# Two groups of tiled matmuls given another place in the order of a recurrent-attention and SoLU kernel

## The chip, the cores and the metric

The kernel runs on one core of one Trainium2 chip. The metric is the device time of one launch in microseconds (us), the median of the runs shown. All arithmetic is in float32.

## What is computed

A gated linear recurrence over 768 tokens, for 4 batches of 8 heads of width 48, is followed by a feed-forward block on the 3072 resulting rows of width 384. The block projects to 1024 (`w_in`), weighs by a softmax, normalises, and projects back to 384 (`w_out`).

```python
for t in range(S):
    state = alpha[:, :, t, :, None] * state + np.einsum('bhd,bhe->bhde', k[:, :, t], v[:, :, t])
    y[:, :, t] = np.einsum('bhd,bhde->bhe', q[:, :, t], state)
...
h = x @ w_in
e = np.exp(h - h_max)
sm = e / (np.sum(e, axis=-1, keepdims=True) + 1e-09)
solu = h * sm
ln = (solu - mu) / np.sqrt(var + 1e-06) * g_ln
return ln @ w_out
```

## The kernel before

The 768 tokens are cut into G = 6 groups of 128. Within a group the recurrence is turned into matrix products: decayed queries times decayed keys give scores, the scores are masked, and the output y is the masked scores times the values plus a read of the state that the earlier groups left. A product of keys and values then brings the state forward to the next group.

The order of instructions is written out by hand, since the tile scheduler is set to manual. Each engine works off its own instructions in program order. From line 922 on, the kernel goes through periods g = 1 to 5, each of 8 steps s. In each step, the feed-forward block of group g is driven on by one eighth (`up(g, s)`: three matmuls from x through `w_in` into a bank `h`, line 394, then Exp on ScalarE at line 408, a product on VectorE at 409 and Square on ScalarE at 412), one half of a projection back of an earlier group is done (`down`, eight matmuls, line 507), and the parts of the attention of group a = g + 1 are put in between. Dictionaries say which part goes where: `first` for period 1 and `usual` for periods 2, 3 and 4 (period 5 has no attention left). The places in a step are, in order: head, then `up` and `finish` (the output of a projected block: small sums on VectorE, a power on GpSimd at line 546, the scaled copy on ScalarE at 548, the store on SP at 549), then `next_state` and `token_sums` where step 0 has them, then behind, `running` (sums kept by VectorE and GpSimd, line 427), middle, `down`, tail.

The parts that matter here:

- `read_state(half)`, called "read0" and "read1" in the plans: half of the read of the state, 32 matmuls of 64 rows by 32 columns of the array (line 333, from `state` and the queries `q64` in the tile `lot`) into four banks y of PSUM.
- `read_values(a)`, "values": 64 matmuls of 128 rows by 32 columns (line 333, from masked scores `sT` and values `vn`) into the same banks; after them four copies on ScalarE (line 363) bring y into `x`, which `up(a, 0)` reads.
- `next_state(a)`, "kv": 64 matmuls of 128 rows by 32 columns (line 371, keys `kg` and values `vn`) into two of the banks that y had; then two sums on VectorE (line 381) into `state`.
- `token_sums(g - 1)`: 16 matmuls of 128 rows by 32 columns (line 462), the row sums of the feed-forward block's running sums, then a transposition and small sums on VectorE (lines 467 to 473).
- `down` and `up` use the whole array, 128 rows by 128 columns.

An instruction in float32 shows as two matmul records in the trace, so `up` is 6 records, `down` 8 for a half (it issues four instructions of 128 by 385), a half read 64, values 128, kv 128, the row sums 32.

In the kernel before, for periods 2, 3 and 4, read0 is in the middle of step 6, read1 in the tail of step 6 (behind `down`), and values in the middle of step 7 (behind `up(g, 7)`). In period 1, read1 and values already stand together in the middle of step 7. `next_state(1)` and `next_state(2)` are called at step 0 of their own periods, behind `up(g, 0)`; `next_state(3)` and `next_state(4)` are called as "kv" in the tail of step 7 of periods 2 and 3, behind `down` and ahead of the next period's `up(g, 0)`. `load_v(a)`, four loads on SP into `vn` (line 176), stands behind step 0, so it comes after the product that reads the values of the group before.

Of the kernel before, what the change touches and what calls it, by code (L numbers as in the profile page):

```python
# [32 lines left out]
def fast_path(ctx, tc, q, k, v, alpha, moe_w_in, moe_w_out, moe_g_ln, out):  # L33
# [97 lines left out]
    def load(src, dst, g):  # L131
        t = slice(g * P, (g + 1) * P)
        for b in range(B):
            nc.sync.dma_start(
                out=dst[32 * b : 32 * b + 32].rearrange("t h u d -> t h (u d)"),
                in_=src[b, :, t, :].rearrange("h (t u) d -> t h (u d)", u=TQ),
            )
# [35 lines left out]
    def load_v(g):  # L173
        t = slice(g * P, (g + 1) * P)
        for b in range(B):
            nc.sync.dma_start(out=held(vn, b), in_=v[b, :, t, :].rearrange("h p d -> p h d"))

    def firsts(src, dst):
        nc.vector.transpose(out=dst.rearrange("p h (t u) -> p h u t", u=TQ), in_=src[:, :, :, 0:E0])  # L179

    def lasts(src, dst):
        nc.vector.transpose(
            out=dst.rearrange("p j (i t u) -> p u j i t", u=TQ, i=2),
            in_=src[:, :, :, E0:D].rearrange("p (j i) u d -> p u j i d", i=2),
        )

    def alpha_T(g):
        nc.gpsimd.memset(aT[:, :, 0:1], 0.0)
        firsts(an, aT[:, 0:H, 1:SW])
        lasts(an, aT[:, H:NB, 1:SW])  # L190
# [15 lines left out]
    def scan_back(g, i):  # L206

        part = slice(NP * i, NP * i + NP)
        scan(h4[:, part], aT[:, part], unit, True)

    def inverses(g):
        nc.gpsimd.tensor_copy(out=fend[:, g], in_=h4[:, :, 1])  # L212
        nc.vector.reciprocal(out=seed[:, :, 0:1], in_=h4[:, :, 1:2])

    def scan_on(g, i):
        part = slice(NP * i, NP * i + NP)
        scan(aT[:, part], aT[:, part], seed[:, part], False)

    def keys_T(g):
        firsts(kn, kT[:, 0:H])  # L220
        lasts(kn, kT[:, H:NB])

    def keys(g):
        for part in (slice(0, H), slice(H, NB)):
            nc.gpsimd.tensor_tensor(out=kT[:, part], in0=kT[:, part], in1=hk[:, part], op=ALU.mult)  # L225

    def move_lasts():

        for b in range(B):
            i, c = divmod(b, 2)  # L230
            for k in range(2):
                nc.sync.dma_start(out=q64[64 * i + E0 : 64 * i + 64, c, k::2], in_=qe[32 * b : 32 * b + 32])

    def move_firsts():
        for b in range(B):
            i, c = divmod(b, 2)
            nc.sync.dma_start(out=q64[64 * i : 64 * i + E0, c], in_=qv[32 * b : 32 * b + 32, 0:H])

    def ends_of_decay():
        nc.gpsimd.tensor_copy(out=qe[:, :, P:SW], in_=h4[:, H:NB, 1:2])  # L240
        nc.gpsimd.tensor_copy(out=qv[:, 0:H, P:SW], in_=h4[:, 0:H, 1:2])

    def apart():
        for i in range(2):
            nc.scalar.mul(
                out=qv[:, H : 2 * H, 0:P].rearrange("p (j i) t -> p j i t", i=2)[:, :, i], in_=qe[:, :, 0:P],
                mul=parity[:, i : i + 1],
            )

    def queries(i):  # L250
        part = slice(NP * i, NP * i + NP)
        q = qe[:, :, 0:P] if i == 2 else qv[:, part, 0:P]
        nc.gpsimd.tensor_tensor(out=q, in0=q, in1=aT[:, part, 1:SW], op=ALU.mult)

    def decay(g):

        if g == 0:
            return
        for c in range(2):
            x = held(state, c)  # L260
            nc.gpsimd.tensor_tensor(  # L261
                out=x, in0=x, in1=q64[:, c, :, P:SW].to_broadcast([P, H, D]), op=ALU.mult
            )
# [22 lines left out]
    def masked(half, batches=range(B)):  # L286
        a = masks[half]
        for b in batches:
            nc.vector.tensor_tensor(  # L289
                out=sT[:, b, half * NP : half * NP + NP], in0=a[b], in1=mask[:, None, :].to_broadcast([P, NP, P]),  # L290
                op=ALU.mult,
            )
# [7 lines left out]
    def keys_back(g, t=None):  # L300
        t = t or banks("tp", [NP, P], 3)
        for j in range(NB):
            nc.tensor.transpose(out=t[j // NP][:, j % NP], in_=kT[:, j], identity=ident)
        for i in range(2):
            nc.scalar.copy(
                out=kg[:, :, NP * i : NP * i + NP, 0:E0].rearrange("p b j d -> p j b d"),
                in_=t[i].rearrange("p j (b d) -> p j b d", b=B),
            )
        for m in range(2):
            nc.scalar.copy(  # L310
                out=kg[:, :, m::2, E0 + E1 * m : D + E1 * m].rearrange("p b j d -> p j b d"),
                in_=t[2].rearrange("p j (b k d) -> p j b k d", b=B, k=2)[:, :, :, m],
            )
# [521 lines left out]
    for i in range(3):  # L835
# [11 lines left out]
    usual = dict(  # L847
        head={4: "keys_back", 5: "masked0", 6: "masked1"},
        behind={0: "v keys", 1: "on2 on0 on1", 2: "lasts firsts", 3: "apart", 5: "decay", 6: "alpha", 7: "back"},
        middle={6: "begin read0", 7: "values"},  # L850
        tail={4: "scores0", 5: "scores1", 6: "read1", 7: "kv"},
    )
    first = dict(
        head={3: "keys_back"},
# [4 lines left out]
        tail={6: "begin read0"},  # L859
        middle={7: "read1 values over"},  # L860
    )

    def attend(a, what):

        more = a + 1 < G
        if what == "v":
            load_v(a)
        elif what == "keys":
            keys_T(a)
            keys(a)  # L870
            if more:
                load(k, kn, a + 1)
        elif what[:2] == "on":
            if what == "on2":
                inverses(a)
            scan_on(a, int(what[2]))
        elif what == "lasts":
            lasts(qn, qe[:, :, 0:P])
            ends_of_decay()
            queries(2)  # L880
            move_lasts()
        elif what == "firsts":
            firsts(qn, qv[:, 0:H, 0:P])
            queries(0)
            queries(1)
            move_firsts()
            if more:
                load(q, qn, a + 1)
        elif what == "apart":
            apart()  # L890
        elif what == "decay":
            decay(a)
        elif what == "keys_back":
            if more:
                keys_back(a)
        elif what[:6] == "scores":
            scores(a, int(what[6]))
        elif what[:6] == "masked":
            masked(int(what[6]))
        elif what == "alpha" and more:  # L900
            alpha_T(a + 1)
            if a > 2:
                attend(a, "over")
        elif what == "over" and more:
            alpha_over(a + 1)
            if a + 2 < G:
                load(alpha, an, a + 2)
        elif what == "back" and more:
            for i in range(3):
                scan_back(a + 1, i)  # L910
        elif what == "begin":
            read_begin()
        elif what[:4] == "read":
            read_state(int(what[4]))
        elif what == "values":
            read_values(a)
        elif what == "kv" and more:
            next_state(a)

    centres = {4: (0, 1), 6: (2, 3), 7: (4, 5, 6, 7)}  # L920
# [1 line left out]
    for g in range(1, G + 1):  # L922
        rise, att = g < G, g + 1 < G
        plan = first if g == 1 else usual

        def at(where, s):
            for what in plan[where].get(s, "").split() if att else ():
                attend(g + 1, what)

        after = 3 if g == 1 else None  # L930
        if not rise:
            break
        for s in range(FC):
            at("head", s)
            if rise:
                up(g, s)
            if after is not None:
                finish(after)
                after = None
            if s == 0 and g < 3:  # L940
                next_state(g)
            if s == 0 and g > 1:
                token_sums(g - 1)
            at("behind", s)
            for f in centres.get(s, ()) if g == 1 else ():
                centre(f)
            if rise and s:
                running(g, s)
            at("middle", s)
            if s == FC - 1 and g < G - 1:  # L950
                todo.append((g * B, 0))
            if todo:
                n, half = todo.pop(0)
                down(n, half)
                if half:
                    after = n
            at("tail", s)
        if after is not None:
            finish(after)
        todo = [(n, half) for n in range(g * B, g * B + B) for half in range(2)][g < G - 1 :]  # L960
# [493 lines left out]
```

## Time and profile before

| | |
|---|---|
| median of 3 runs | 368.86 us (368.79 to 369.36) |
| the profiled execution's own time | 369.21 us |
| its span, first to last instruction | 367.4 us |
| TensorE (PE) busy | 359.7 us, 98% |
| VectorE (DVE), ScalarE (ACT), GpSimd (POOL) busy | 245.4, 146.1, 131.1 us |
| `down`, line 507, all periods | 384 records, 134.0 us |
| `up`, line 394, all periods | 288 records, 132.1 us |
| values, line 333 | 768 records, 22.6 us |
| read of the state, line 333 | 640 records, 11.6 us |
| kv, line 371 | 640 records, 7.8 us |

How to read it: the profile is of one execution, and its span leaves out 1.8 us of that execution's own time, which lie around the first and the last instruction. A line of the list in order of time gives the start of a group in us from the span's start, its length, the engine, the source line, the tile written and those read, then for TensorE the rows and columns of the array that are used (128\*128 is the whole array), the shape of the moving operand, and the number of records. What stands in brackets at the end is the time that the engine sat idle before, and who ended it. PEld is TensorE's weight load, listed as an engine of its own. Matmuls are pipelined and their ends are modelled, so the starts are the firm numbers.

### The profile page before, as it was taken

The page shows a single profiled execution, that of the slowest core. Times are in us where ns is not written, and L with a number is a line of the kernel's source. Part 1 is how long each engine was busy: PE and PEld are TensorE (multiplying, and loading weights), DVE is VectorE, ACT ScalarE, POOL GpSimd, SP SyncE. Part 2 cuts the span into 40 slices and gives each one's busy share as a digit, 9 for nine tenths or more (in the row PEclk, how much of TensorE's full clock was granted, in tenths as well). Part 3 has the DMA queues.
Part 4 walks back from the last instruction along what each step waited for, and adds up shares of the span by engine and source line. Part 5 has one row for each costly group of instructions (what it writes and reads, how often), then busy time and mean ns, then how long its engine had stood idle before and what let it go on. Part 6 is the DMA issues. An engine that isn't in the chain of part 4 may idle for free. (4 is left out here: it accounts for less than half of the span.)

```text
span 367.4 us, 10036 instructions
## 1 busy us (share of the span) xinstructions
PE 359.7 (98%) x4341; PEld 215.9 (59%) x4341; DVE 245.4 (67%) x375; ACT 146.1 (40%) x260; POOL 131.1 (36%) x129
## 2 busy tenths in 40 slices
PE   8999999999999999999999999999999999999994
PEld 8885355676755566566575556574556565555552
DVE  0999999979998787936575935665956314345420
ACT  2647878282645262251432252431242132222110
POOL 7020000004449944763133764232774121233300
PEclk9999999999999999999999999999999999999999
DMA  9996986335196419363135354004042000000011
GB/s 181 186 317 181 220 269 130 87 82 144 53 229 146 105 29 184 77 154 86 33 80 118 75 129 118 4 23 87 21 101 60 2 23 0 24 21 22 23 46 51
DMA packets 72871, 36.06 MB, mean 98 GB/s; under 512 B 48232, under 2 KB 70000, under 8 KB 72816
## 3 DMA queue, kind: packets, MB, share of 16 engines
q1 hardware_dynamic: 71792, 34.39, 39.8%
q10 hardware_dynamic: 1024, 0.92, 0.8%
q8 instruction: 36, 0.59, 0.7%
q14 instruction: 19, 0.16, 0.1%
HBM read 25.30 MB, written 4.72 MB: 82 GB/s over the span
## 5 line engine op out<-in xcount | busy, mean ns | idle before, releaser
L507 PE MATMUL o<-w_out,room 128*128 128x385 f32 x384 | 134.0, 492 | 0.0
L394 PE MATMUL h<-x,w_in 128*128 128x512 f32 x288 | 132.1, 598 | 0.5 <-DVE g_col L642 0.5
L507 PEld LDWEIGHTS o<-w_out,room 128*128 128x128 f32 x384 | 71.0, 190 | 54.7 <-issue 13.1
L394 PEld LDWEIGHTS h<-x,w_in 128*128 128x128 f32 x288 | 52.9, 189 | 58.2 <-issue 49.1
L409 DVE TENSOR_TENSOR room<-h,e 128x512 f32<-128x512 f32 x40 | 27.5, 688 | 73.7 <-ACT e L408 73.7
L408 ACT ACTIVATE e<-h 128x512 f32<-128x512 f32 x40 | 24.0, 599 | 100.6 <-PE h L394 100.6
L427 POOL TENSOR_TENSOR p<-p,e 128x512 f32<-128x512 f32 x30 | 42.7, 1423 | 20.0 <-ACT e L408 19.9
L412 ACT ACTIVATE u<-room 128x512 f32<-128x512 f32 x40 | 25.2, 630 | 39.3 <-DVE room L409 39.3
L546 POOL TENSOR_TENSOR r<-sums,mhalf 128x1 f32<-128x1 f32 x20 | 14.8, 739 | 72.9 <-DVE sums L537 72.7
L289 DVE TENSOR_TENSOR sT<-a,mask 128x512 f32<-128x512 f32 x43 | 26.7, 683 | 7.7 <-PE a L278 7.6
L204 DVE TENSOR_TENSOR_SCAN hT<-aT,unit 128x516 f32<-128x516 f32 x18 | 24.0, 1376 | 8.1 <-ACT aT L703 8.1
L204 DVE TENSOR_TENSOR_SCAN aT<-aT,seed 128x516 f32<-128x516 f32 x18 | 27.4, 1551 | 0.2
L427 DVE TENSOR_TENSOR p<-p,u 128x512 f32<-128x512 f32 x30 | 23.1, 768 | 5.1 <-ACT u L412 5.1
L225 POOL TENSOR_TENSOR kT<-kT,hT 128x1024 f32<-128x1024 f32 (+1 forms) x8 | 14.2, 1796 | 32.6 <-DVE kT L179 32.6
L278 PEld LDWEIGHTS a<-qv,kT 32*128 32x128 f32 x704 | 21.4, 186 | 7.4 <-issue 2.4
L278 PE MATMUL a<-qv,kT 32*128 32x128 f32 x704 | 23.9, 278 | 0.9 <-DVE qv L721 0.4
L212 POOL COPY fend<-hT 128x12 f32<-128x12 f32 x6 | 3.0, 507 | 56.1 <-DVE hT L204 56.1
L333 PE MATMUL y<-sT,vn 128*32 128x128 f32 x768 | 22.6, 273 | 0.2 <-DVE sT L289 0.2
L333 PEld LDWEIGHTS y<-sT,vn 128*32 128x32 f32 x768 | 20.7, 110 | 3.3 <-issue 2.7
L196 ACT ACTIVATE sq<-an,mone 128x1536 uint8<-128x1536 f32 x12 | 18.9, 1573 | 0.2
L548 ACT ACTIVATE o_sb<-o,r 128x384 f32<-128x384 f32 x16 | 9.3, 581 | 18.7 <-POOL r L546 18.7
L261 POOL TENSOR_TENSOR state<-state,lot 128x384 f32<-128x384 f32 x10 | 8.8, 900 | 12.0 <-DMA lot<-qv 11.8
(148 smaller groups left out, 375.8 us busy)
## 6 DMA issues: line engine op xcount, KB each, us to landing
vn<-in_v_dram SPq DMA_DIRECT2D x24, 192.0 KB, 4.6
an<-in_alpha_dram SPq DMA_DIRECT2D x20, 192.0 KB, 3.8
out_dram<-o_sb SPq DMA_DIRECT2D x20, 192.0 KB, 1.9
room<-in_moe_w_out_dram SPq DMA_DIRECT2D x8, 384.0 KB, 5.0
kn<-in_k_dram SPq DMA_DIRECT2D x16, 192.0 KB, 4.8
qn<-in_q_dram SPq DMA_DIRECT2D x16, 192.0 KB, 3.8
lot<-qe SPq DMA_DIRECT2D x40, 64.5 KB, 2.1
lot<-qv SPq DMA_DIRECT2D x20, 129.0 KB, 2.4
```

What stands on the lines that cost most here:

```text
L196: nc.scalar.activation(out=sq, in_=x, func=AF.Relu, scale=sign, bias=mone, accum_out=over[:, g, i : i + 1])
L204: nc.vector.tensor_tensor_scan(out=o, data0=a, data1=s, initial=1.0, op0=ALU.mult, op1=ALU.add)
L278: nc.tensor.matmul(a[b][:, i], lhsT=kT[quarter(b), kb], rhs=qv[quarter(b), qb, 0:P], start=not last and not i, stop=bool(last), tile_posit ...
L289: nc.vector.tensor_tensor(out=sT[:, b, half * NP : half * NP + NP], in0=a[b], in1=mask[:, None, :].to_broadcast([P, NP, P]), op=ALU.mult,)
L333: nc.tensor.matmul(y_bank(b)[quarter(r), a], lhsT=lhsT, rhs=rhs, start=(b, r) not in begun, stop=stop, tile_position=(row, 32 * r), skip_g ...
L394: nc.tensor.matmul(h, lhsT=w_in[:, a, f * P : (f + 1) * P], rhs=d["x"][:, a].rearrange("p b t -> p (b t)"), start=(a == 0), stop=(a == KC ...
L408: nc.scalar.activation(out=e, in_=h, func=AF.Exp)
L409: nc.vector.tensor_tensor(out=u, in0=h, in1=e, op=ALU.mult)
L412: nc.scalar.activation(out=u2, in_=u, func=AF.Square)
L427: eng.tensor_tensor(out=p, in0=d[0][i] if f == 1 else p, in1=d[f][i], op=ALU.add)
L507: nc.tensor.matmul(d["o"][:, 0 : DM + 1], lhsT=u_of(g, f)[:, b * P : b * P + P], rhs=w_out[:, f], start=(f == 0), stop=(f == FC - 1), skip ...
L546: nc.gpsimd.tensor_tensor(out=r, in0=s[:, 3:4], in1=mhalf, op=ALU.pow)
```

## The change

In the plan `usual`, "read1" goes from the tail of step 6 to the middle of step 7, right ahead of "values". So in periods 2, 3 and 4 the second half of the read comes behind `down` of step 6 and `up(g, 7)`. For group 4 alone, `next_state` is no longer called in the tail of step 7 of period 3 but at step 0 of period 4, behind `up(4, 0)` and right ahead of `token_sums(3)`. No instruction is added, removed or changed in shape.

```diff
     usual = dict(
         head={4: "keys_back", 5: "masked0", 6: "masked1"},
         behind={0: "v keys", 1: "on2 on0 on1", 2: "lasts firsts", 3: "apart", 5: "decay", 6: "alpha", 7: "back"},
-        middle={6: "begin read0", 7: "values"},
-        tail={4: "scores0", 5: "scores1", 6: "read1", 7: "kv"},
+        middle={6: "begin read0", 7: "read1 values"},
+        tail={4: "scores0", 5: "scores1", 7: "kv"},
     )
...
-        elif what == "kv" and more:
+        elif what == "kv" and more and a != 4:
             next_state(a)
...
-            if s == 0 and g < 3:
+            if s == 0 and g in (1, 2, 4):
                 next_state(g)
             if s == 0 and g > 1:
                 token_sums(g - 1)
```

## Prediction

> **What bounds the kernel now.** I read first the page's share of each engine, then TensorE's list in order of time over the later periods, then the same list where period g=1 ends, then ScalarE's and GpSimd's lists around one seam.
>
> ```profile
> PE 359.7 (98%) x4341; PEld 215.9 (59%) x4341; DVE 245.4 (67%) x375; ACT 146.1 (40%) x260; POOL 131.1 (36%) x129
> ```
>
> TensorE is busy all the time and nothing else is near it; the wait table gives it 0.2 to 1.1 us at seven places, none of them after 114 us. So the end moves one for one with the time from one TensorE group's start to the next group's start. I use starts throughout, since the ends are modelled and overlap the next start by 0.07 to 0.17 us.
>
> The seam of g=3 into g=4, before the change:
>
> ```profile
> 231.99 1.16 PE L333 MATMUL y<-lot,state 64*32 64x128 f32 x64
> 233.08 2.86 PE L507 MATMUL o<-w_out,room 128*128 128x385 f32 x8
> 235.87 1.16 PE L333 MATMUL y<-lot,state 64*32 64x128 f32 x64
> 236.96 2.84 PE L394 MATMUL h<-x,w_in 128*128 128x512 f32 x6
> 239.73 3.70 PE L333 MATMUL y<-sT,vn 128*32 128x128 f32 x128
> 243.36 2.86 PE L507 MATMUL o<-w_out,room 128*128 128x385 f32 x8
> 246.15 1.57 PE L371 MATMUL kv<-vn,kg 128*32 128x48 f32 x128
> 247.65 2.84 PE L394 MATMUL h<-x,w_in 128*128 128x512 f32 x6
> 250.42 0.65 PE L462 MATMUL rows<-p,ones 128*32 128x64 f32 x32
> 251.00 2.86 PE L507 MATMUL o<-w_out,room 128*128 128x385 f32 x8
> 253.70 2.74 PE L394 MATMUL h<-x,w_in 128*128 128x512 f32 x6
> 256.28 2.76 PE L507 MATMUL o<-w_out,room 128*128 128x385 f32 x8
> ```
>
> The fifth column is the shape of the array: 128*128 is whole, 64*32 or 128*32 is tiled. Look at how a whole-array group's length depends on its neighbours. Up (L394) takes 256.28 - 253.70 = 2.58 between two whole groups, 2.77 between two tiled ones (236.96 to 239.73, 247.65 to 250.42). Down (L507) takes 2.79 between two tiled ones (233.08, 243.36), 2.70 with only the group ahead tiled (251.00), and 2.59 to 2.60 between whole ones (the same list at 256.28 and 261.44). Each border between shapes costs about 0.1 us at either side of a whole group.
>
> Where g=1 ends, the kernel of before already has both orders that the change makes:
>
> ```profile
> 127.12 1.16 PE L333 MATMUL y<-lot,state 64*32 64x128 f32 x64
> 128.21 3.70 PE L333 MATMUL y<-sT,vn 128*32 128x128 f32 x128
> 131.84 2.86 PE L507 MATMUL o<-w_out,room 128*128 128x385 f32 x8
> 134.54 2.74 PE L394 MATMUL h<-x,w_in 128*128 128x512 f32 x6
> 137.21 1.57 PE L371 MATMUL kv<-vn,kg 128*32 128x48 f32 x128
> 138.59 0.64 PE L462 MATMUL rows<-p,ones 128*32 128x64 f32 x32
> 139.16 2.86 PE L507 MATMUL o<-w_out,room 128*128 128x385 f32 x8
> ```
>
> The read takes 1.09 with values behind it, as against 1.09 with up behind it (235.87 to 236.96); values take 3.63 in both places. The product kv takes 1.38 ahead of the row sums and 1.50 ahead of up.
>
> **What the Trainium skill says.** TensorEngine Tiling (Array Packing), section Key Properties: "Mode switching requires drain", a change of the tiling mode and not of the tile. It gives no price; this trace agrees and gives about 0.1 us at each side of a whole group. TensorE: Matmul & The Clock Gate, section Step-by-step: what each phase is for, says that TensorE pulls a weight load ahead of matmuls in flight. The list of weight loads agrees: between whole groups the load of up starts at 253.38, 0.32 ahead of its matmul at 253.70; behind a tiled group it starts together with its matmul, at 236.96; so what a border costs may be this lead. Perfetto Trace Analysis, section Identifying the Most-Contended Engine, says that TensorE's busy share is a poor measure because matmuls are pipelined: the 98% does not say that nothing can be gained, and indeed the same six matmuls take 2.58 or 2.77.
>
> **Part 1: the read of the state moved behind up of step 7** (periods g=2, 3, 4). Nothing is added or removed: 64 matmul records (32 instructions) trade places with the 6 of up. Before, from the start of down at step 6 to the end of values: 2.79 + 1.09 + 2.77 + 3.63 = 10.28, and the window sums show 10.28 for 177.16:187.44, 233.08:243.36 and 287.69:297.97 alike. After: down with a tiled group ahead and a whole one behind, 2.70 (251.00 and 131.84); up with a whole one ahead and a tiled one behind, 2.67 (134.54); read ahead of values, 1.09; values 3.63. Sum 10.09. Gain 0.19 each, 0.57 for three. It is free of new waits if up can start 1.18 earlier (1.09 + 0.09): its bank h was given up by step 5, and its Exp sat idle 2.44 us waiting for it at 239.84. VectorE sat idle 3.52 before its product at 240.47. What read waits for (queries in q64, the state decayed by GpSimd) is older still than for the first read. Values come no earlier relative to the masks; DVE's masks precede the first read anyway, since both use the same banks.
>
> **Part 2: next_state(4) moved out of step 7 of g=3 to behind up of step 0 of g=4**, once. Before, from the start of down to the end of the row sums: 2.79 + 1.50 + 2.77 + 0.58 = 7.64 (243.36 to 251.00; also 7.64 at 187.44 to 195.08). After it is the order at g=2, step 0: 2.70 + 2.67 + 1.38 + 0.57 = 7.32 (131.84 to 139.16). Gain 0.32.
>
> What else moves with it: two VectorE sums L381 (0.55 each) now stand behind the product L409 of up and ahead of the transposition of the row sums, as at 138.00, 138.78 and 139.72, where TensorE lost nothing. The state is wanted next by decay at step 5. On SP the four loads of v for period 5 wait for kv to have read vn: their issue slips from 247.66 by about 2.5 us relative to the seam (kv ends 6.75 behind the end of values instead of 4.29). Behind them on SP is the output store issued at 259.78, 6 us past their new end, and values want vn only at 294. GpSimd's queue keeps its order.
>
> The cover that gets thinner is x. Up of step 0 needs the four ScalarE copies of y (L363), and kv no longer stands between:
>
> ```profile
> 243.13 0.58 ACT L548 ACTIVATE o_sb<-o,r 128x384 f32<-128x384 f32 x1 [1.31 <-POOL r L546]
> 243.61 1.61 ACT L363 COPY x<-y 128x384 f32<-128x384 f32 x4
> ```
>
> The copies end at 245.22, 1.86 behind the end of values, held up by an output step that waits for GpSimd's 1.40 us power. Up will now come 2.70 behind the end of values instead of 4.29. That still leaves 0.84; and since up of step 7 runs 1.18 earlier against values, its whole chain (Exp, product, finish, power, output) does too, so the copies should end some 0.6 behind values and the slack be near 2. At g=4 the kernel of before already starts up 2.70 behind values (297.97 to 300.67), copies ending 1.06 behind, without a wait. I take nothing; from below it cannot be a gain, and from above, if all ScalarE work slipped by 1.5 us, it would cost 0.7.
>
> **Sum.** 0.57 + 0.32 = 0.89. Starts are read to 0.01, four seams of two readings each: 0.85 to 0.93. Behind each seam every group goes on at its usual length up to the last store, with no wait that could swallow the gain. The profiled execution took 369.21 for a span of 367.4, so it would become 368.32 with a span of 366.5; the median before is 368.86, 0.35 under that execution, so the forecast median is 367.97. That is 0.24% off, and this kernel's times can tell about 0.2% (0.74 us) from no change, so the sign is surer than the class.
>
> **The rivals.**
> - The borders save less where they now stand (64*32 straight into 128*32 is read from one place only, g=1, with both groups there under other loads), or x costs some: half to two thirds of the sum, 368.3 to 368.4. For it: one sample per new order. Against: the old orders repeat to 0.01 in three periods, so lengths hardly depend on what other engines do.
> - Up of step 0 waits for x at the seam from g=3 to g=4, and the end is later. Place: L394 at step 0 of g=4. Price: one for one past 2.70 behind values, so the copies would have to end 2.70 + 0.89 + 0.74 = 4.33 behind values to make it slower by 0.2%; then 369.6 or more. For it: ScalarE's output step there waits on a GpSimd power of 1.40 us beside VectorE's scans (0.55 at g=4). Against: it takes 2.5 us more than now, and the chain starts 1.18 earlier.
> - The change does not do what it says: the program's order of instructions has the moves on TensorE and on VectorE (L381) and none on GpSimd or SP; the time would stay 368.86. Very unlikely.
>
> **How the numbers follow.** Forecast 0.80, part of the gain 0.15, waiting for x 0.03, no effect 0.02. The forecast falls on the near side of 0.74 in about one of eight medians (the three before spread over 0.57): 0.70 of faster, 0.10 of same. Same adds the partial case and no effect less a little for noise: 0.26. Slower 0.04. The range runs from 367.5 (0.89 and a low median) to 368.65, which takes in the partial case.
>
> **What would show it.** Right: in g=2, 3, 4 the order down, up, read, values with 2.70, 2.67, 1.09, 3.63; at g=4 step 0 up, kv, rows with 2.67, 1.38, 0.57; span near 366.5. Wrong: up of step 0 in g=4 starting more than 2.71 behind values; the read longer than 1.10 ahead of values; a new TensorE wait in the table; or a later group longer than before, so that the gain is given back.

## The result and the profile after

The changed kernel took 368.08 us (median of 12 runs, 367.89 to 369.74) against 368.90 for the kernel before (12 runs, 368.77 to 370.30). The ratio is 0.9978, with a 95% interval of 0.9969 to 0.9987: 0.22% faster, and by that interval between 0.13% and 0.31%. Timed once more in the last group of experiments (label e12_changed_again), the ratio was 0.9971 (0.9960 to 0.9982). So it is faster by both intervals; whether by more than the 0.2% at which the forecast drew its line they leave open.

The profiled execution took 367.97 with a span of 366.2. TensorE's list in order of time shows the seam of g=3 into g=4 as it now is; the columns are those shown before.

```profile
231.53 1.16 PE L333 MATMUL y<-lot,state 64*32 64x128 f32 x64
232.63 2.86 PE L507 MATMUL o<-w_out,room 128*128 128x385 f32 x8
235.32 2.74 PE L394 MATMUL h<-x,w_in 128*128 128x512 f32 x6
237.99 1.16 PE L333 MATMUL y<-lot,state 64*32 64x128 f32 x64
239.08 3.70 PE L333 MATMUL y<-sT,vn 128*32 128x128 f32 x128
242.71 2.86 PE L507 MATMUL o<-w_out,room 128*128 128x385 f32 x8
245.41 2.74 PE L394 MATMUL h<-x,w_in 128*128 128x512 f32 x6
248.07 1.57 PE L371 MATMUL kv<-vn,kg 128*32 128x48 f32 x128
249.47 0.65 PE L462 MATMUL rows<-p,ones 128*32 128x64 f32 x32
250.05 2.86 PE L507 MATMUL o<-w_out,room 128*128 128x385 f32 x8
```

From start to start (down is line 507, up 394, kv 371, the row sums 462): down 2.69, up 2.67, read 1.09, values 3.63, together 10.08 in place of 10.28; then down 2.70, up 2.66, kv 1.40, row sums 0.58, together 7.34 in place of 7.64. In period 2 the first sum is 10.09 (176.90 to 186.99), in period 4 it is 10.08 (286.74 to 296.82); both were 10.28 before.

ScalarE's list around the same seam, for the cover of x:

```profile
241.39 0.58 ACT L548 ACTIVATE o_sb<-o,r 128x384 f32<-128x384 f32 x1 [1.31 <-POOL r L546]
241.87 1.61 ACT L363 COPY x<-y 128x384 f32<-128x384 f32 x4
```

The copies end at 243.48, 0.77 behind the end of values, and up follows at 245.41, 2.70 behind: no wait.

To compare single executions I use one stretch in what follows: from the start of the row sums of period 2 to the start of the last matmul of down. All that the change moves lies inside it, and the loads at the start lie outside; in every trace kept here the granted clock is 1.00 all through it. It was 223.41 us before and is 222.52 now: 0.90 less by the unrounded figures. The two spans differ by 1.24. Of the rest, 0.25 came earlier than 127 us and 0.09 behind the last matmul of down; nothing is changed in either place, so I take it for a difference between two executions.

### The profile page after: what moved, and what is told of

Read it like the earlier page. It is cut to its first block, busy times and chain, and to the rows that moved or that the text cites. A ratio compares the mean times of both kernels' runs of the same rounds, so it can differ in the third digit from the quotient of the medians.

```text
span 366.2 us, 10036 instructions
## 1 busy us (share of the span) xinstructions
PE 357.8 (98%) x4341; PEld 215.0 (59%) x4341; DVE 245.0 (67%) x375; ACT 146.4 (40%) x260; POOL 132.2 (36%) x129
## 5 line engine op out<-in xcount | busy, mean ns | idle before, releaser
L427 POOL TENSOR_TENSOR p<-p,e 128x512 f32<-128x512 f32 x30 | 43.7, 1458 | 20.0 <-ACT e L408 19.9
```

The costliest lines, as they stand in the source:

```text
L427: eng.tensor_tensor(out=p, in0=d[0][i] if f == 1 else p, in1=d[f][i], op=ALU.add)
```

## Experiments

The theory under test is the border theory: what counts is how often TensorE passes between groups of different array shape. The first rival is that up's earlier start did it; the others are waits (for x, or at the row sums). All experiments were timed against the kernel before on the same chip; the table gives each one's stretch too, which is that of a single execution.

| run | median us | ratio to before, 95% interval | stretch us |
|---|---|---|---|
| changed kernel | 368.08 | 0.9978 (0.9969 to 0.9987) | 222.52 |
| e1_read_alone | 368.51 | 0.9984 (0.9976 to 0.9991) | 222.82 |
| e2_kv_alone | 368.74 | 0.9991 (0.9981 to 1.0001) | 223.10 |
| e3_values_split | 369.13 | 1.0001 (0.9993 to 1.0009) | 223.51 |
| e4_rows_first | 368.20 | 0.9968 (0.9956 to 0.9981) | 222.52 |
| e5_kv3 | 368.14 | 0.9969 (0.9955 to 0.9982) | 222.26 |
| e6_reads_joined | 368.38 | 0.9978 (0.9970 to 0.9986) | 222.59 |
| e7_x_uncovered | 369.14 | 1.0000 (0.9990 to 1.0010) | 223.35 |
| e8_all_joined | 368.26 | 0.9974 (0.9964 to 0.9983) | 222.93 |
| e9_joined_34 | 367.48 | 0.9951 (0.9936 to 0.9966) | 221.44 |
| e10_shifted | 368.95 | 0.9997 (0.9985 to 1.0009) | 223.07 |
| e11_alpha_later | 368.21 | 0.9977 (0.9966 to 0.9988) | 222.92 |
| e12_changed_again | 368.26 | 0.9971 (0.9960 to 0.9982) | 222.58 |

### Each part alone

Part 1 alone (to the kernel before):

```diff
-        middle={6: "begin read0", 7: "values"},
-        tail={4: "scores0", 5: "scores1", 6: "read1", 7: "kv"},
+        middle={6: "begin read0", 7: "read1 values"},
+        tail={4: "scores0", 5: "scores1", 7: "kv"},
```

> Part 1 alone: the second read moved ahead of values in periods 2, 3 and 4, the product kv for group 4 left where it was. Border theory (what counts is how often TensorE goes between whole-array and tiled groups, about 0.10 us at each side of a whole group and 0.11 at the end of a tiled one): 10.28 becomes 10.09 in each of the three periods, 0.57 us less than before, nothing at the seam from g=3 to g=4 (7.64 stays). Earlier-start theory (the gain comes from step 7's up starting 1.2 us earlier for ScalarE and VectorE, the order of shapes being idle): no number for TensorE's groups, which would keep 2.79, 2.77 and 1.09, and a gain only where a wait was, so 0.

Part 2 alone (to the kernel before):

```diff
-        elif what == "kv" and more:
+        elif what == "kv" and more and a != 4:
...
-            if s == 0 and g < 3:
+            if s == 0 and g in (1, 2, 4):
```

> Part 2 alone: kv for group 4 behind up of step 0 and ahead of the row sums, the read left in step 6. Border theory: 7.64 becomes 7.32 at the seam from g=3 to g=4, 0.32 us less than before, 10.28 stays in all three periods; and the four copies of x end about 1.86 us behind values, so up at 2.70 behind still does not wait. Waiting-for-x theory: without part 1 the cover of x is thinner, up starts later than 2.71 behind values, and the gain is below 0.32.

The stretch became 0.59 and 0.31 shorter, for 0.57 and 0.32 expected, and the two add up to the 0.90 of both. In e1, TensorE had no wait before or after the change in these periods and still gained, which the earlier-start theory can't give.

TensorE's list of e2, from the end of values:

```profile
243.83 2.86 PE L507 MATMUL o<-w_out,room 128*128 128x385 f32 x8
246.53 2.74 PE L394 MATMUL h<-x,w_in 128*128 128x512 f32 x6
249.19 1.57 PE L371 MATMUL kv<-vn,kg 128*32 128x48 f32 x128
250.58 0.64 PE L462 MATMUL rows<-p,ones 128*32 128x64 f32 x32
251.15 2.86 PE L507 MATMUL o<-w_out,room 128*128 128x385 f32 x8
```

Up of step 0 came 2.70 behind values (243.83 to 246.53), so the smaller cover of x was enough even without part 1. By the times alone, part 2 would not be told from no change (the interval reaches 1.0001); the trace shows it (7.32 from 243.83 to 251.15, where it was 7.64).

### A border put back

```diff
-        middle={6: "begin read0", 7: "read1 values"},
+        middle={6: "begin read0", 7: "read1 values01"},
...
+        elif what == "values01":
+            read_values(a, (0, 1))
...
-                down(n, half)
+                if s == FC - 1 and att and g > 1:
+                    down(n, half, (0, 1))
+                    read_values(g + 1, (2, 3))
+                    down(n, half, (2, 3))
+                else:
+                    down(n, half)
```

> The changed kernel with a border put back: in step 7 of periods 2, 3 and 4, values of batches 0 and 1, half of down, values of batches 2 and 3, the other half of down. Same instructions, one more trip from tiled to whole and back in each period. Border theory: 0.10 + 0.10 at the whole group and 0.11 at the end of the tiled one, 0.31 us each, 0.94 in all above the changed kernel, so about 369.0, level with before. Earlier-start theory: no instruction of up moves, so nothing, 368.1.

TensorE's list of that kernel, from values to up of step 0:

```profile
239.16 1.96 PE L333 MATMUL y<-sT,vn 128*32 128x128 f32 x64
241.04 1.56 PE L507 MATMUL o<-w_out,room 128*128 128x385 f32 x4
242.53 1.95 PE L333 MATMUL y<-sT,vn 128*32 128x128 f32 x64
244.42 1.56 PE L507 MATMUL o<-w_out,room 128*128 128x385 f32 x4
245.82 2.74 PE L394 MATMUL h<-x,w_in 128*128 128x512 f32 x6
```

The same matmuls took 6.66 (239.16 to 245.82) where the changed kernel needs 6.33 (239.08 to 245.41). The two halves of values take 1.88 and 1.89, 0.14 more than the whole; the two halves of down 1.49 and 1.40, 0.19 more. Three times 0.33 is 0.99, and the stretch is 0.99 longer; the time is back level with before. No instruction of up was moved, so the earlier-start theory can't explain the loss; with e1 it has fallen.

### The same borders in another order

```diff
-            if s == 0 and g in (1, 2, 4):
+            if s == 0 and g in (1, 2):
                 next_state(g)
             if s == 0 and g > 1:
                 token_sums(g - 1)
+            if s == 0 and g == 4:
+                next_state(g)
```

> The changed kernel with the row sums ahead of kv at step 0 of period 4 in place of behind it. The same borders in another order. Border theory: the same time as the changed kernel, up 2.67, row sums about 0.46 (no border behind them), kv 1.50 (a border behind it), their sum 1.95 as before. A theory by which kv has to stand ahead of the row sums (its banks, or the sums' wait for the running sums of step 7): a wait of TensorE there, and longer.

TensorE's list of that kernel:

```profile
248.13 0.65 PE L462 MATMUL rows<-p,ones 128*32 128x64 f32 x32
248.60 1.54 PE L371 MATMUL kv<-vn,kg 128*32 128x48 f32 x128
250.07 2.86 PE L507 MATMUL o<-w_out,room 128*128 128x385 f32 x8
```

The stretch is the same to 0.01. The row sums take 0.47 with kv behind them (248.13 to 248.60) in place of 0.58, and kv 1.47 with down behind it in place of 1.40: the end of a tiled group costs about 0.1 when the next group has another array shape, and whichever of the two is last pays it. It is the adjacency that counts and not the place of kv.

### The cover of x

In period 3 down of step 7 is left out of its place and called in period 4 behind up of step 0:

```diff
             if rise:
                 up(g, s)
+            if g == 4 and s == 0:
+                down(3 * B, 0)
...
-                down(n, half)
+                if not (g == 3 and s == FC - 1):
+                    down(n, half)
```

> The changed kernel with the cover of x taken away at the seam from g=3 to g=4: down goes behind up of step 0, so that values are followed at once by up. The shapes and their borders are as many as before. Wait-for-x theory: up starts when the fourth copy of x is done, about 0.77 us behind values plus up to 0.1, so some 0.8 to 0.9 us longer than the changed kernel. No-wait theory: the same time.

TensorE's list of that kernel:

```profile
238.85 3.70 PE L333 MATMUL y<-sT,vn 128*32 128x128 f32 x128
243.31 2.84 PE L394 MATMUL h<-x,w_in 128*128 128x512 f32 x6 [0.76 <-ACT x L363]
245.99 2.76 PE L507 MATMUL o<-w_out,room 128*128 128x385 f32 x8
```

Up could have started at 242.48, 3.63 behind the start of values, and started 0.83 later, at once behind the copies of x, which end at 243.26 in ScalarE's list. The stretch is 0.83 longer. So the price of the forecast's second rival is real and one for one; it is down's 2.70 that hides it, and in the changed kernel 1.9 us of that are spare.

### Further in the same direction

The product for group 3 treated like that for group 4:

```diff
-        elif what == "kv" and more and a != 4:
+        elif what == "kv" and more and a < 3:
...
-            if s == 0 and g in (1, 2, 4):
+            if s == 0 and g in (1, 2, 3, 4):
```

> The changed kernel with kv for group 3 treated as that for group 4: at step 0 of period 3, behind up and ahead of the row sums. Border theory: 7.64 becomes 7.32 at the seam from g=2 to g=3 as well, 0.32 us less than the changed kernel. A theory by which group 3 is left out because it would wait (loads of k for group 5 stand behind the loads of v on SP in that period and start about 2.5 us later): a wait of TensorE later in period 3, and no gain or a loss.

The seam of g=2 into g=3 took 7.32 (188.85 to 196.17), 0.32 less as expected, and TensorE had no later wait in that period. The stretch is only 0.26 shorter, since kv of group 4 took 1.46 in this execution where it took 1.40 in the changed kernel's; why its length scatters from 1.38 to 1.46 is not shown. The times do not tell it from the changed kernel.

The first read moved as well:

```diff
-        middle={6: "begin read0", 7: "read1 values"},
+        middle={7: "begin read0 read1 values"},
```

> The changed kernel with the first read moved too, so that in periods 2, 3 and 4 up of step 7 is followed by both reads and values. One border pair less at up of step 6 and down of step 6, and none between the two reads, which have the same shape. Full border theory (a tiled group pays 0.11 at its end for any change of shape, even to another tiled shape): 0.20 at the whole groups and 0.11 between the reads (the first read takes 0.98, the second still 1.09 ahead of values), 0.31 us each, 0.92 in all below the changed kernel. Whole-array-only theory (only borders with whole-array groups cost): the first read keeps 1.09, 0.20 each, 0.6 in all.

TensorE's list of that kernel, period 3:

```profile
237.48 2.04 PE L333 MATMUL y<-lot,state 64*32 64x128 f32 x128
239.46 3.70 PE L333 MATMUL y<-sT,vn 128*32 128x128 f32 x128
243.09 2.86 PE L507 MATMUL o<-w_out,room 128*128 128x385 f32 x8
```

and period 2:

```profile
180.92 2.04 PE L333 MATMUL y<-lot,state 64*32 64x128 f32 x128
182.89 1.07 PE L333 MATMUL y<-sT,vn 128*32 128x128 f32 x26
184.80 3.04 PE L333 MATMUL y<-sT,vn 128*32 128x128 f32 x102 [0.84 <-issue]
187.77 2.86 PE L507 MATMUL o<-w_out,room 128*128 128x385 f32 x8
```

In period 3 the two reads take 1.98 together; with 1.09 for the second, the first takes 0.89, which is 0.20 less than with a border behind it. The whole-array-only theory has fallen: two tiled groups of different shape, read and values, also have a border to pay, and it costs more than the 0.11 that I had put in. From up of step 6 to the end of values it is 13.55 (229.54 to 243.09) in place of 13.95 (228.76 to 242.71): 0.40 a period. But the kernel as a whole gained nothing over the changed one. In period 2, after 26 records of values, TensorE stood still for no wait that the profile names (it writes "issue"): values took 4.88 (182.89 to 187.77) in place of 3.63, 1.25 more, which eats three times 0.40.

Everything together, with period 1's first read joined too:

```diff
-        middle={6: "begin read0", 7: "read1 values"},
+        middle={7: "begin read0 read1 values"},
...
-        tail={6: "begin read0"},
-        middle={7: "read1 values over"},
+        tail={},
+        middle={7: "begin read0 read1 values over"},
...
-        elif what == "kv" and more and a != 4:
+        elif what == "kv" and more and a < 3:
...
-            if s == 0 and g in (1, 2, 4):
+            if s == 0 and g in (1, 2, 3, 4):
```

> The changed kernel with kv for group 3 at step 0 as well and the two reads joined ahead of values in periods 1 to 4. Full border theory: 0.32 and four times 0.31, 1.56 us less than the changed kernel, so 366.5. Whole-array-only theory: 0.32 and four times 0.2, 1.1 less, 367.0. If ScalarE, which does the range sums of alpha in step 6 and 7, then comes too late with Exp of step 7 for the next up, a wait of TensorE shows at up of step 1 and part is lost.

It took 368.26 for 366.5 expected. The gap of period 2 came at the same record again and was longer (values 5.46, 182.76 to 188.22), and in period 1 values took 4.02 (127.38 to 131.40) in place of 3.63. There was no wait for ScalarE; what I had named as the danger was not what happened.

### What the gaps are

I counted TensorE's records from the start of each trace, beginning with 0: weight loads, matmuls and the 58 semaphore and control records that the views leave out. The gap in period 2 of e6 and of e8 stands ahead of record 5313. That is 193 + 20 x 256. The page of the kernel before lists among the DMA queues one of kind instruction with 36 packets of 0.59 MB in all, 16 KB each (q8; the page's other one, q14, has 19), and the Trainium skill, page Perfetto Trace Analysis, section The 4-stage abstract model, gives 64 bytes for an instruction: 256 in a packet. Together that is room for 9216 instructions, and TensorE has 8740 records, far more than any other engine, so I took q8 for TensorE's, and the gap for a block of instructions that had not come in time. In e6 the only packet of q8 near the gap starts at 182.21 and takes 1.20. The reads, with values behind them, had begun at 180.92, and 256 records of reads pass in about 2 us. The DMA view of that kernel, from 180.9 to 184.0 us:

```profile
q1 hardware_dynamic: 516, 0.37, 47.7%
q8 instruction: 1, 0.02, 2.4%
...
an<-in_alpha_dram SPq DMA_DIRECT2D x4, 192.0 KB, 4.1
```

One instruction packet, among 516 of the four alpha loads: so those could be the cause too. Two kernels were to tell the block's place from the loads. The first shifts the whole stream by 56 records (to e6):

```diff
+            if g == 1 and s == 2:
+                t = ps_o.tile([P, 512], FP, tag="o", name="shift")
+                for i in range(14):
+                    nc.tensor.matmul(t[0:1, 0:1], lhsT=ones[:, 0:1], rhs=ones[:, 0:1], start=True, stop=True)
             at("behind", s)
```

> The kernel with joined reads in periods 2, 3 and 4, and 14 one-column matmuls (56 instruction records, some 0.5 to 1 us of TensorE) put in at step 2 of period 1; their result is not used. Instruction-block theory: the border of the block moves from 26 matmuls into the values of period 2 to their start, and the block behind it is asked for some 5 us earlier, during up and down; so the gap of 1.1 us in the values of period 2 is gone (3.63 in place of 4.87). In period 4 the margin gets thin, a gap of up to 0.2 may come. Load theory (the loads of alpha at 181 us take the DMA engines from the instruction fetch): the gap stays.

The second moves the loads (to e6; for group 5 the load is called at step 0 of period 3):

```diff
-            if a + 2 < G:
+            if a + 2 < G and a != 3:
                 load(alpha, an, a + 2)
...
+            if s == 0 and g == 3:
+                load(alpha, an, 5)
             at("behind", s)
```

> The kernel with joined reads in periods 2, 3 and 4, with the loads of alpha for group 5 put behind the output store on SP, so that they start at about 185.3 and not at 181.2 us. Load theory: the instruction packet of 182.2 us travels alone, and the gap in the values of period 2 is gone. Instruction-block theory: the block is asked for no earlier, so most of the gap stays (1.0 or a little less; a packet alone may take 0.3 us less).

TensorE's list of the shifted kernel in period 2:

```profile
183.25 3.70 PE L333 MATMUL y<-sT,vn 128*32 128x128 f32 x126
187.69 0.41 PE L333 MATMUL y<-sT,vn 128*32 128x128 f32 x2 [0.74 <-issue]
188.03 2.86 PE L507 MATMUL o<-w_out,room 128*128 128x385 f32 x8
```

and of the kernel with alpha later:

```profile
182.72 1.07 PE L333 MATMUL y<-sT,vn 128*32 128x128 f32 x26
184.86 3.04 PE L333 MATMUL y<-sT,vn 128*32 128x128 f32 x102 [1.07 <-issue]
187.83 2.86 PE L507 MATMUL o<-w_out,room 128*128 128x385 f32 x8
```

With alpha later the instruction packet travelled without the loads (it started at 181.94, they at 185.20), and the gap stayed, 1.07: the loads are not its cause. With the shift the old gap was gone, 126 records of values ran through, but my expectation of no gap was wrong: a new one of 0.74 came ahead of record 5569, the next border of a block, and in period 4 values took 4.17 (293.43 to 297.60) where I had allowed for 0.2 more. The gap follows the block and not the place in the program. The 0.54 more in period 4 hold a shorter delay of the same kind, ahead of record 8129 (193 + 31 x 256), and the 0.39 more in period 1 of e8 one ahead of 4033 (193 + 15 x 256).

The traces also show what the record behind a gap waits for. Counted in order, from the first packet in the trace for the block at record 449 on, the packets go with the blocks one for one. In all eleven gaps of more than 0.5 us (listed at the end) that packet is the last to start before the gap ends, and the record behind the gap starts 1.30 to 1.60 us after the packet's end. Over all 14 traces, 33 blocks each, no block begins less than 1.25 us after the end of its packet. By these figures a gap comes where a block is used up before the next one's packet is that far behind. Speed alone doesn't decide it: in e9, below, kv and the row sums use up the block from record 5569 in 1.40 us without a gap, since the next packet had started at 190.41, 2.2 us before that block began (192.62). In e10 the packet for 5569 started only at 185.47, 2.43 behind the start of the block ahead of it; why it was so late is not settled (the alpha loads were under way then).

The last kernel takes what gains without a gap: kv of group 3 as in e5, reads joined in periods 3 and 4 alone.

```diff
+    joined = dict(usual, middle={7: "begin read0 read1 values"})
...
-        plan = first if g == 1 else usual
+        plan = first if g == 1 else usual if g == 2 else joined
```

> The changed kernel with kv for group 3 at step 0 too, and the two reads joined ahead of values in periods 3 and 4 only, where the joined runs before showed no gap. From the groups measured: 0.32 for kv, 13.95 to 13.55 (0.40) for each joined period, 1.1 us less than the changed kernel, so about 367.0; from the row sums of period 2 to the last matmul 221.4 in place of 222.5. Instruction-block theory (gaps come where TensorE uses up a block of 256 instructions in less than about 3 us): none in these two periods, since the block that ends there is asked for while up and down of steps 6 and 7 run. If gaps come at random in dense stretches, some of the gain is lost.

TensorE's list of that kernel, period 3:

```profile
236.52 2.04 PE L333 MATMUL y<-lot,state 64*32 64x128 f32 x128
238.50 3.70 PE L333 MATMUL y<-sT,vn 128*32 128x128 f32 x128
242.13 2.86 PE L507 MATMUL o<-w_out,room 128*128 128x385 f32 x8
```

The stretch is 221.44 for 221.4 expected, 1.08 below the changed kernel, with no gap in periods 2 to 4. The expectation's figure, a block used up in less than about 3 us, is not the border between gap and no gap: the 1.40 us named above are in this kernel. The median is 367.48, the ratio to before 0.9951 (0.9936 to 0.9966): the fastest of all. The changed kernel timed beside it as a control:

> The changed kernel itself, on the same chip as the three with it, to compare against: ratio 0.9978 to before, from the row sums of period 2 to the last matmul 222.5 us, no gap in the values of period 2.

It gave 368.26 and a stretch of 222.58, with no gap in the values of period 2. It had one of 1.14 at the start, at 24.64 us in the values of group 0, ahead of record 961, which is 193 + 3 x 256.

## Why the prediction was right

- **The bound.** TensorE's start-to-start times set the end; 0.89 forecast, 0.90 in the stretch, 0.82 between the medians. The medians of the kernel before alone, timed with each group of experiments, run from 368.86 to 369.08, so a median can't confirm the hundredths; the stretch does. That the ratio came out on the far side of 0.2% owes something to luck, as the forecast's own chances said.
- **Part 1**, 2.70 + 2.67 + 1.09 + 3.63: found to 0.01 in all three periods, 0.59 by e1.
- **Part 2**, 7.32: measured 7.34 in the changed kernel and 7.32 in e2 (243.83 to 251.15); kv took 1.40 in place of 1.38 in the one and 1.39 in the other. The values loads on SP began at 249.59, 6.88 behind the end of values where about 6.75 was worked out, and nothing waited for them.
- **Nothing for x.** The copies ended 0.77 behind values where some 0.6 was forecast. The sum there was off: up of step 7 comes 1.18 earlier against the seam, but its end comes only 1.09 earlier against values, by the read that now stands between, and 1.86 - 1.09 is 0.77. The value taken, nothing, was right because of down's 2.70; e7 shows what it would have cost without down, 0.83. The forecast's bound (0.7, if ScalarE's work slipped by 1.5) was not tested by any run.
- **The rivals.** That the borders save less in their new place fell with the repeated sums (the order of read and values had a second sample in the list before, 90.91 to 91.99, with 1.08, where the forecast counts only one); the wait for x did not come; that nothing changes fell with the ratio.
- **A slip in reading.** The array's shape is the seventh entry of a line in those lists, not the fifth; no number hangs on it.
- **The mechanism.** The forecast read only that lengths depend on neighbours. e3 shows that a border put in costs about what one taken out gains (0.33 a period, against 0.32 for part 2); e4 that the order of kv and the row sums as such costs nothing. The drain that the Trainium skill names at a change of mode (TensorEngine Tiling, section Key Properties) agrees with all of them, also with the border between two tiled shapes in e6. The forecast's other thought, that the price may be the lost lead of the weight load, wasn't separated from a drain by any run.

What the forecast did not look at is that going on in this direction has a limit of another kind, which this change stays just short of: in the changed kernel's trace record 6849, in the values of period 3, starts without a gap, but only 1.44 us after the end of its packet, where the least found in any trace is 1.25.

## What to carry to other kernels

Where TensorE is the bound, list the start-to-start lengths of its groups by their neighbours' shapes: a trip from the whole array to a tile shape and back that was saved brought 0.3 to 0.4 us here where the tiled groups joined had the same shape (kv and row sums, the two reads), and 0.2 where they had not (read and values, which still pay a border between them). A good order groups the same shapes as far as buffers and waits allow. A place in the same trace where the new order already stands gave the price to 0.02. But long runs of small matmuls use up instructions fast: after joining them, look for gaps with no releaser, and count records, semaphore records too, to see whether the gaps stand a multiple of 256 apart.

## What the runs showed of the hardware

- A border costs about 0.10 us at each side of a whole-array group, and at the end of a tiled group 0.11 (row sums, e4), 0.12 (kv, before), 0.14 (values, e3) and 0.20 (read, e6) if the next array shape is another; for the read it is the same whether that is a tiled shape or the whole array (1.09 in both places before).
- The instruction packets of q8, 16 KB each, take 0.88 to 2.86 us, and no block of 256 begins less than 1.25 us after the end of its packet, counted in order. All eleven unnamed gaps of more than 0.5 us (start to start) inside a group in these traces stand at record 193 plus a multiple of 256: 961 (six executions), 1473 (e5), 5313 (e6, e8, e11), 5569 (e10). Two of these places, at 23 and 35 us, every kernel has: a gap is there in one execution and not in the next, from 0.5 to 1.5 us long. That may be part of why executions of the same kernel differ by more than this change brings; the runs were not made to test that.
- In e6, 2.6 us went by from the start of the packet at 182.21 to the record behind the gap, at 184.80, of which the packet's own time is 1.2; no other packet came before the gap ended.
